# A fused attention, expert and feed-forward kernel: everything from the second expert on written twice, with smaller static blocks in the copy that a flag from the token counts picks

## Chip, cores and metric

The kernel runs on one core of one Trainium2 chip. The metric is device time in microseconds (us). One core has TensorE (PE; its weight loads are shown as PEld), VectorE (DVE), ScalarE (ACT), GpSimd (POOL), SyncE (SP, which issues transfers here) and 16 DMA engines. [...]

## What is computed

Attention with a threshold, then a layer of eight experts in which every token goes to one expert, then a gated feed-forward network. Cut to what matters here:

```python
scores = scale * q @ k.T                       # 4 batches, 8 heads, 576 tokens, 64 wide
scores = where(scores >= max(scores) - tau, scores, -1e9)
x = (softmax(scores) @ v)                      # -> x: 2304 tokens x 512
logits = x @ w_gate                            # 2304 x 8
expert = argmax(logits, axis=1)
for e in range(8):
    xe = x[expert == e]
    y[expert == e] = prob[expert == e] * (maximum(xe @ w1[e], 0) @ w2[e])   # 512 -> 1024 -> 512
h = y @ w_in                                   # 512 -> 2048
out = (h * sigmoid(1.702 * h)) @ w_out         # 2048 -> 512
```

How many tokens an expert gets is known only when the kernel runs. With the inputs used here the reference's routing gives, sorted, 535, 339, 305, 270, 267, 218, 197 and 173 tokens.

## The kernel before

**Stages.** `attention` runs first and also does the gate. Its last steps, in `count` (which calls `routing` and `offsets`), sort the experts by their number of tokens: rank 0 is the expert with most. While attention still runs, the kernel picks the expert that leads so far and does its first 256 tokens as rank 0's first block (`first_ops`); `Moe1.ahead` prepares the remaining `CAPS[0] - FIRST` = 304 columns of rank 0. Then `Moe1.plan` does those 304 columns and one block for each of ranks 1 to 7, and `Moe2.plan` the feed-forward network in six blocks of 384 tokens.

**Static blocks.** Matmul widths are fixed when the program is built. Rank r has a block of `CAPS[r]` columns: 544, 448, 376, 336, 312, 288, 264, 256. Columns beyond the tokens that are there are padding rows. If a rank has more tokens than its block, a general path (`general`) adds further blocks of 256 in a loop; the value `trip`, computed in `offsets` and loaded into a register of every engine by `load_trip`, says whether it is needed. `tc.If(trip > 0)` stands between attention and `Moe1.plan`, and here every engine jumps over its body.

**One block.** Each weight and activation is split in two parts, high and low (type float32r, `F32R`), and every product is done as three matmuls (high x high, high x low, low x high). A block of n columns has 96 matmuls for `x @ w1` (line 1243: 8 chunks of 128 hidden features, 4 input chunks, 3 products) and 96 for `h @ w2` (line 1259), all with a 128 x 128 weight and n columns. A block's tokens come as gathers of 128 rows (`XCH`), each followed by a group of four transposes on TensorE (line 1234) and two copies (`put_x`). Weights of an expert come as eight pieces of 512 KB (`load_w`, line 1224) through three buffers `wraw`; ScalarE copies the high part (line 1389) and VectorE subtracts for the low part (line 1393): a split. `reg_op` and `idx_op` fetch a rank's expert number, offset and index list on SyncE. In the free time of the other engines 32 jobs convert `w_in` from 64-bit numbers (`wi_job`, `convert64`), as 16 more convert `w_out` in the second network.

**Order.** The whole order is written out by hand through a planner (`Plan`): each operation has an engine, a cost, a key and dependencies. `Plan.order` always takes the operation that can start first, by the costs given, and the smaller key where two can start at once; rings (`pl.ring`) stand for buffers. The operations are then emitted in that order, and each engine works through its own list strictly in order. All of attention, `ahead` and `first_ops` are one such list, all of `Moe1.plan` and `Moe2.plan` another. An `If` splits lists: nothing of one side can be moved past it, and each engine passes it when it gets there.

**Memory.** In `moe_kernel` the pools `ht`, `w0`, `xt`, `y`, `wiraw`, `cv`, `cv1` and `w1` serve the experts and are closed (`c2.close`) when `Moe2.open` opens its own: `wo2`, `yg` (four buffers for x loads), `cv2`, `x2_p`, `wo1`, `gp` and `t`. Outputs leave through three buffers `xg`, one indirect scatter of 128 rows at a time on GpSimd (line 1676).

Of the kernel before, what the change touches and what calls it, by code (L numbers as in the profile page):

```python
# [22 lines left out]
SEG = 2560  # L23
TBR = E * SEG
CAPS = [544, 448, 376, 336, 312, 288, 264, 256]
XW = 2 * NT + 256
# [21 lines left out]
class Plan:  # L48
# [11 lines left out]
    def op(self, eng, cost, key, fn, deps=(), take=None, free=None, lat=None, after=(), halves=False):  # L60
# [11 lines left out]
        return o  # L72

# [934 lines left out]

XCH = [[min(o, c - 128) for o in range(0, c, 128)] for c in CAPS]
XCH[0] = [min(o, CAPS[0] - 128) for o in range(FIRST, CAPS[0], 128)]  # L1010
NBLK = [[(0, 256), (FIRST, CAPS[0] - FIRST)]] + [[(0, c)] for c in CAPS[1:]]
HW = max(n for bl in NBLK for _, n in bl)
TB = 384
NC_CONST = 8 * 3 + 9 + 64 + 8


def shape_consts():
# [7 lines left out]
    c[:, 97] = BIG / 8  # L1025
    c[:, 33:97] = (np.arange(8)[None, :] < np.arange(8)[:, None]).reshape(64)
# [61 lines left out]
def offsets(nc, st, sm):  # L1088
# [19 lines left out]
    nc.vector.tensor_reduce(trip, nb, axis=AX.X, op=ALU.max)  # L1108
    before = sm.tile([128, E, E], F32, name="before")
# [16 lines left out]
    st.update(offi=offi, trip=trip, nbi=nbi, row0=row0, col0=col0)  # L1126


def load_trip(nc, st):
    st["trip_v"] = nc.values_load(st["trip"][0:1, 0:1], min_val=0, max_val=7)  # L1130
# [132 lines left out]
class Moe1:  # L1263


    def __init__(self, nc, st, ex):
        self.nc, self.st, self.ex, self.P = nc, st, ex, ex.P
        self.regs, self.offs, self.raws, self.wts = {}, {}, {}, {}
        self.idx, self.xgs, self.xts, self.xt, self.h = {}, {}, {}, {}, {}
        self.ops, self.all_st = {}, []  # L1270

# [3 lines left out]
    def w(self, r, which, k):  # L1275
        return self.wts[(r, which, k)] if r else self.st["first"]["w"][(which, k)]
# [12 lines left out]
    def idx_op(self, pl, r, key, deps):  # L1289
        nch, r0, dma = len(XCH[r]), XCH[r][0], self.nc.sync.dma_start  # L1290
        full = (CAPS[r] - r0) // 128
        rows = lambda: self.st["tb"][bass.ds(self.reg(r) * SEG + r0, CAPS[r] - r0)]

# [4 lines left out]
        def part():  # L1298
            dma(self.idx[r][:, full, :], rows()[CAPS[r] - r0 - 128 : CAPS[r] - r0])
# [22 lines left out]
    def ahead(self, pl, bank_of, tiles, h_op):  # L1322
# [5 lines left out]
        n = NBLK[0][1][1]  # L1328
        ops[("x", 0)] = []
        prev = []  # L1330
        for i in range(len(XCH[0])):
            self.gather_op(pl, 0, i, key, st["all_stores"])
            x, r0 = XCH[0][i], XCH[0][0]
# [29 lines left out]
    def plan(self, pl, wi_job, after):  # L1363
        nc, st, ex, P, ops = self.nc, self.st, self.ex, self.P, self.ops
        K = KEYS1
        self.offs[0] = 0
        for name, n in (("w0", 4), ("w1", 4), ("xt", 1), ("y", 3), ("wiraw", 2), ("cv", 2), ("cv1", 1)):
            pl.ring(name, n)
        pl.banks = {k: [(i,) for i in range(8)] for k in "THY"}
        pl.psum = [max(pl.now["ACT"], pl.now["DVE"])] * 8  # L1370
        bank = lambda t, n: self.banks[t["k"][0]][:, 0:n]
        T = T0 = pl.now["PE"]
        prev_y, stores, ids_prev = {}, [], []
        blocks = [NBLK[0][1]] + [b[0] for b in NBLK[1:]]
        times = []
        for off, n in blocks:
            times.append((T, T + 96 * n / 2400 + 0.25))
            T += 192 * n / 2400 + 0.5

        def split(r, which, k):  # L1380
# [20 lines left out]
        def put_x(r, i):  # L1401
            t = times[r][0]
            tx, tp = ops[("xt", r)], {}
            if ("gather", r, i) not in ops:
                self.gather_op(pl, r, i, t - K["G"], [])
            x, r0 = XCH[r][i], XCH[r][0]
# [6 lines left out]
            def hi():  # L1413
                if i == 0:
                    xt = self.xt[r] = [P["xt"].tile([128, 4, HW], F32R, name=nm) for nm in ("xh", "xl")]
# [19 lines left out]
        o_off = pl.op("ACT", 0.3, times[6][0], last_off)  # L1435

        for r, (off, n) in enumerate(blocks):
            last = r == E - 1
# [3 lines left out]
            if r:  # L1442
# [4 lines left out]
                for k in range(4):  # L1447
                    split(r, 0, k)
            if r:
                ops[("xt", r)] = {}  # L1450
                for i in range(len(XCH[r])):
                    put_x(r, i)
# [5 lines left out]
            for fc in range(8):  # L1458
# [5 lines left out]
                def h_hi(fc=fc, tp=tp, r=r, n=n):  # L1464
                    self.h[r][fc] = [P["ht"].tile([128, HW], F32R, name=f"{p}{fc}")[:, 0:n] for p in ("hh", "hl")]
# [61 lines left out]
            def ids(r=r):  # L1527
                src = st["tb"][bass.ds(self.reg(r) * SEG, CAPS[r])]
                nc.sync.dma_start(st["tbc"][bass.ds(self.offs[r], CAPS[r])], src)

            ids_prev = [pl.dma(ty + 14 * c, 0.1, [ids], [ops[("reg", r)]] + ids_prev, after=[o_y])]

        before, late = pl.ops[:first_y], pl.ops[first_y:]
# [11 lines left out]
def general(tc, nc, st, w):  # L1545
# [7 lines left out]
    with tc.If(st["trip_v"] > 0), ExitStack() as c:  # L1553
        pool = c.enter_context(tc.tile_pool(name="gen", bufs=1))
        ps = c.enter_context(tc.tile_pool(name="ps_g", bufs=2, space=PSUM))
        with tc.For_i(0, E, 1) as r:
            reg, row0, col0 = load("kidx", r, E - 1), load("row0", r, (E - 1) * SEG + CAPS[0]), load("col0", r, NT + CAPS[0])
            nb = nc.values_load(st["nbi"][0:1, bass.ds(r, 1)], min_val=0, max_val=7)
            with tc.For_i(0, nb, 1) as k:
# [10 lines left out]
                for i in range(2):  # L1570
# [4 lines left out]
                    t_ps = ps.tile([128, 4, 128], F32, name="gt")  # L1575
# [4 lines left out]
                for fc in range(8):  # L1580
                    h_ps = ps.tile([128, 256], F32, name="ghp")
# [5 lines left out]
                for dc in range(4):  # L1587
                    y_ps = ps.tile([128, 256], F32, name="gyp")
# [6 lines left out]

class Moe2:
    def __init__(self, tc, nc, st, banks, wi_t, wo, out, raw_p, o_p):
        self.tc, self.nc, self.st, self.banks, self.wi_t, self.wo, self.out = tc, nc, st, banks, wi_t, wo, out
        self.raw_p, self.o_p = raw_p, o_p
        self.xgs, self.x2, self.raws, self.th, self.g, self.ot = {}, {}, {}, {}, {}, {}  # L1600
        self.ids = st["cst"].tile([128, NT // 128, 2], I32, name="ids")

    def open(self, ctx):
        for name, bufs in (("wo2", 1), ("yg", 4), ("cv2", 2), ("x2_p", 1), ("wo1", 1), ("gp", 3), ("t", 2)):
            setattr(self, name, ctx.enter_context(self.tc.tile_pool(name=name, bufs=bufs, reuse_waits="tile")))
        self.wo_t = {}
        for p, Fs in ((self.wo2, range(8, 16)), (self.wo1, range(8))):
            for F in Fs:
# [278 lines left out]
```

## Time and profile before

| what | value |
|---|---|
| timed runs: median (lowest to highest of 3) | 977.88 us (977.53 to 980.33) |
| profiled execution: its own time | 984.31 us |
| profiled execution: span, first to last instruction | 982.6 us |
| granted TensorE clock, mean over the span | 0.987 |
| TensorE busy | 954.6 us, 97% |
| VectorE, ScalarE, GpSimd busy | 562.9, 529.7 and 411.2 us |
| bytes moved by DMA | 106.90 MB, 109 GB/s on average |

The profile is one execution; its time is a little above the timed runs. "Busy" of an engine is time in which it had an instruction under way; waiting and issuing transfers don't count. Matmuls overlap, so that a single one's duration is longer than the distance from one to the next.

### The profile page before, as it was taken

How to read it: one execution, taken by the hardware profiler on the slowest of the kernel's cores; microseconds unless marked ns; L12 is line 12 of the kernel's file. 1: busy time of each engine (PE TensorE's matmuls, PEld its weight loads, DVE VectorE, ACT ScalarE, POOL GpSimd, SP SyncE). 2: the span in 40 equal slices, each digit the busy share in tenths (PEclk: the TensorE clock that was granted, in tenths of full speed). 3: DMA queues.
4: the chain of work that ended last, by engine and by line, in shares of the span. 5: the costliest groups of instructions: out<-in, count | busy, mean ns of one | idle time of the engine just before them, and what ended most of it. 6: DMA issues, size and time to landing. Idle time of an engine off the chain costs nothing.

```text
span 982.6 us, 16924 instructions
## 1 busy us (share of the span) xinstructions
PE 954.6 (97%) x6204; PEld 864.9 (88%) x6205; DVE 562.9 (57%) x1189; ACT 529.7 (54%) x1170; POOL 411.2 (42%) x455
## 2 busy tenths in 40 slices
PE   7998999999989899999999999999999999999996
PEld 5888888888879899999999998999999999999995
DVE  6886888888856347888995488882411111111111
ACT  5886889889854345766675465543322322322221
POOL 6979978845275213555450000001432422522321
PEclk7999999999989999999999999999999999999999
DMA  8723532300243567877776373300200100000000
GB/s 309 223 88 109 162 108 79 108 22 22 58 137 108 171 197 217 257 214 235 241 223 212 116 220 86 106 24 13 95 22 1 54 11 1 33 0 1 33 1 33
DMA packets 50551, 106.90 MB, mean 109 GB/s; under 512 B 12816, under 2 KB 22032, under 8 KB 49936
## 3 DMA queue, kind: packets, MB, share of 16 engines
q1 hardware_dynamic: 45632, 93.43, 30.4%
q0 software_dynamic: 4096, 11.56, 3.8%
q8 instruction: 50, 0.82, 0.4%
q10 hardware_dynamic: 736, 0.79, 0.2%
q14 instruction: 37, 0.30, 0.1%
HBM read 87.37 MB, written 18.57 MB: 108 GB/s over the span
## 4 chain that ended last, share of the span: by engine, by line
PE 61%; DVE 2%; DMA 2%; issue 1%; ACT 0%; POOLq 0%; SPq 0%; DVEq 0%; ACTq 0%
PE b L1639 21%; PE b L1666 20%; PE b L1259 12%; PE b L1243 9%; DVE wlo L1393 1%; DMA wraw<-in_w 1%; PE b L1234 1%; DMA out<-xg,ids 1%; DVE hl L1250 0%; ACT whi L1389 0%; POOLq L1883 0%; DVE wil L1172 0%; ACT xg L1671 0%; ACT yt L1504 0%; ACT hh L1247 0%
## 5 line engine op out<-in xcount | busy, mean ns | idle before, releaser
L1648 DVE SCALAR_TENSOR_TENSOR th<-th,b 128x384 f32<-128x384 f32 x96 | 53.1, 553 | 250.1 <-ACT th L1644 250.1
L1644 ACT ACTIVATE th<-b 128x384 f32<-128x384 f32 x96 | 47.2, 492 | 201.9 <-PE b L1639 198.8
L1639 PE MATMUL b<-x2h,wil 128*128 128x384 f32 x384 | 129.5, 337 | 0.0
L1639 PE MATMUL b<-x2h,wih 128*128 128x384 f32 x384 | 129.3, 337 | 0.0
L1639 PE MATMUL b<-x2l,wih 128*128 128x384 f32 x384 | 128.9, 336 | 0.0
L370 DVE TENSOR_REDUCE nm<-pair 128x1 f32<-128x576 f32 x144 | 107.0, 753 | 27.8 <-PE pair L360 26.2
L389 DVE SCALAR_TENSOR_TENSOR pt<-pair,thr,et 128x576 f32<-128x576 f32 x144 | 114.3, 813 | 13.3 <-ACT et L378 12.3
L1659 POOL TENSOR_TENSOR gl<-th,gh 128x384 fp32r<-128x384 f32 x60 | 61.0, 1017 | 140.1 <-ACT gh L1656 136.3
L1666 PE MATMUL b<-woh,gl 128*128 128x512 f32 x276 | 109.2, 396 | 0.0
L1666 PE MATMUL b<-wol,gh 128*128 128x512 f32 x276 | 109.0, 395 | 0.0
L1666 PE MATMUL b<-woh,gh 128*128 128x512 f32 x276 | 107.3, 389 | 0.0
L378 ACT ACTIVATE et<-pair,nm 128x576 f32<-128x576 f32 x144 | 107.3, 745 | 0.0
L411 ACT COPY ptT<-bank 128x512 f32<-128x512 f32 x144 | 81.3, 589 | 25.4 <-PE bank L405 25.1
L1393 DVE TENSOR_TENSOR wlo<-wraw,whi 128x1024 fp32r<-128x1024 f32 x56 | 75.9, 1375 | 27.1 <-ACT whi L1389 24.1
L405 PE MATMUL bank<-ident,pt 128*128 128x128 f32 x576 | 86.1, 283 | 4.3 <-DVE pt L389 3.3
L1623 POOL TENSOR_TENSOR x2l<-xr,x2h 128x384 fp32r<-128x384 f32 x16 | 16.1, 1033 | 170.5 <-ACT x2h L1619 170.5
L360 PE MATMUL pair<-kst,qh 128*128 128x288 f32 x320 | 84.9, 348 | 1.3 <-DVE kst L285 0.6
L405 PEld LDWEIGHTS bank<-ident,pt 128*128 128x128 f32 x576 | 68.5, 145 | 17.3 <-ACT thr L374 6.2
L1639 PEld LDWEIGHTS b<-x2h,wih 128*128 128x128 f32 x384 | 72.2, 188 | 4.2 <-DVE th L1648 0.3
L1639 PEld LDWEIGHTS b<-x2l,wih 128*128 128x128 f32 x384 | 72.1, 188 | 3.9
L1639 PEld LDWEIGHTS b<-x2h,wil 128*128 128x128 f32 x384 | 72.0, 188 | 0.0
L1259 PE MATMUL b<-hh,whi 128*128 128x448 f32 (+6 forms) x224 | 71.4, 319 | 0.1
(256 smaller groups left out, 2309.6 us busy)
## 6 DMA issues: line engine op xcount, KB each, us to landing
wraw<-in_w SPq DMA_DIRECT2D x64, 512.0 KB, 4.7
qraw<-in_qd SPq DMA_DIRECT2D x40, 256.0 KB, 4.0
wiraw<-in_wi SPq DMA_DIRECT2D x32, 256.0 KB, 4.0
wraw<-in_wo SPq DMA_DIRECT2D x16, 512.0 KB, 3.6
kraw<-in_kd SPq DMA_DIRECT2D x14, 576.0 KB, 4.6
vt<-in_vf SPq DMA_DIRECT2D x4, 1024.0 KB, 7.6
xn<-xt SPq DMA_DIRECT2D x16, 256.0 KB, 3.2
xr<-x2t SPq DMA_DIRECT2D x20, 192.0 KB, 2.7
```

The costliest lines, as they stand in the source:

```text
L360: nc.tensor.matmul(s_ps[:, n, 0:288], w, ks[bb][:, h, 288 * n : 288 * n + 288], start=(i == 0), stop=(i == len(seq) - 1),)
L370: nc.vector.tensor_reduce(t["nm"], t["s"][:, :, 0:288], axis=AX.XY, op=ALU.max, negate=True)
L378: nc.scalar.activation(t["e"], t["s"][:, :, 0:288], AF.Exp, bias=t["nm"], scale=1.0)
L389: nc.vector.scalar_tensor_tensor(pt[:, 576 * x : 576 * x + 576].rearrange("p (n k) -> p n k", n=2), t["s"][:, :, 0:288], t["thr"][:, 0:1], ...
L405: nc.tensor.transpose(t["t"][:, c, :], pt[:, o : o + 128], ident)
L411: nc.scalar.copy(blk["ptT"][:, 4 * x : 4 * x + 4, 128 * ci : 128 * ci + 128], t["t"])
L1243: self.nc.tensor.matmul(h_ps, ww[:, o : o + 128], xx[dc], start=(k == 0), stop=(k == 11))
L1259: self.nc.tensor.matmul(y_ps, w[:, o : o + 128], h, start=(k == 0), stop=(k == 23))
L1393: nc.vector.tensor_tensor(w[1], self.raws.pop((r, which, k)), w[0].bitcast(F32), op=ALU.subtract)
L1639: self.nc.tensor.matmul(h_ps, w[:, dc, :], x[:, dc, :], start=(k == 0), stop=(k == 11))
L1659: eng.tensor_tensor(self.g[n][1], self.th.pop(n), self.g[n][0].bitcast(F32), op=ALU.subtract)
L1666: self.nc.tensor.matmul(o_ps, g[:, cs], w, start=(F == 0 and k == 0), stop=(F == 15 and k == 2))
```

## The change

From rank 1 on, the program stands twice. A second list of widths, `FEW`, is smaller than `CAPS` for all ranks but rank 0. `offsets` computes a flag `more`, which is 1 if any rank has more tokens than `FEW` holds; `load_trip` loads it into a register of every engine in place of `trip`. Rank 0's 304 columns are planned and emitted once, together with what begins rank 1 (its index list, the splits of its first projection and three of its gathers). Then `tc.If(more < 1)` chooses: the first arm plans ranks 1 to 7 and the second network with `FEW`; the other arm first has the general path (moved here from its place after attention) and then the same with `CAPS`. For this, `Plan.fork` and `Moe1.fork` copy the planner's state.

The buffers `ht`, `w0` and `xt` now live from rank 0 to the end, and the second network uses them again: `w0` holds the converted `w_out` of the first eight chunks, `xt` and half of `ht` the two x blocks, the rest of `ht` the gated activations (four buffers instead of three). Its x loads use the three `xg` buffers in place of four of their own.

```diff
+FEW = [544, 384, 344, 320, 304, 280, 256, 232]
...
+    def fork(self):
+        p = copy.copy(self)
+        p.ends = {k: dict(v) for k, v in self.ends.items()}
+        p.ops, p.caps, p.count = list(self.ops), dict(self.caps), dict(self.count)
+        p.psum, p.now = list(self.psum), dict(self.now)
+        p.banks = dict(self.banks)
+        return p
...
+def chunks(caps):
+    return [[min(o, c - 128) for o in range(0 if r else FIRST, c, 128)] for r, c in enumerate(caps)]
...
     nc.vector.tensor_reduce(trip, nb, axis=AX.X, op=ALU.max)
+    nc.vector.tensor_tensor(rest, n, shc[:, 105:113], op=ALU.subtract)
+    over = sm.tile([128, 1], F32, name="over")
+    nc.vector.tensor_reduce(over, rest, axis=AX.X, op=ALU.max)
+    more = cst.tile([128, 1], I32, name="more")
+    nc.vector.tensor_scalar(more, over, 0.0, None, op0=ALU.is_gt)
...
-    st["trip_v"] = nc.values_load(st["trip"][0:1, 0:1], min_val=0, max_val=7)
+    st["more_v"] = nc.values_load(st["more"][0:1, 0:1], min_val=0, max_val=1)
...
-                w = [P[f"w{which}"].tile([128, 1024], F32R, name=x) for x in ("whi", "wlo")]
+                w = [P["w1"].tile([128, 1024], F32R, name=x) for x in ("whi", "wlo")] if which else self.w0[k]
...
-        for name, bufs in (("wo2", 1), ("yg", 4), ("cv2", 2), ("x2_p", 1), ("wo1", 1), ("gp", 3), ("t", 2)):
+        for name, bufs in (("cv2", 2), ("t", 2), ("wo_p", 1)):
...
-        raw = self.yg.tile([128, TB], F32, name="xr")
+        raw = self.o_p.tile([128, DM], F32, name="xg")[:, 0:TB]
...
-        general(tc, nc, st, ex.w)
...
+        def begin(pl, split, put_x):
+            m1.idx_op(pl, 1, 0.0, [])
+            for k in range(4):
+                split(1, 0, k)
+            for i in range(3):
+                put_x(1, i)
+
+        with ExitStack() as c:
+            P["y"] = c.enter_context(tc.tile_pool(name="y0", bufs=3, reuse_waits="tile"))
+            for name, n in (("w0", 4), ("xt", 1), ("y", 3)):
+                pl.ring(name, n)
+            m1.plan(pl, [0], begin)
...
+        with tc.If(st["more_v"] < 1) as fits:
+            with ExitStack() as c:
+                rest(c, pl.fork(), m1.fork(FEW))
+        with fits.Else():
+            general(tc, nc, st, ex.w, banks)
+            with ExitStack() as c:
+                rest(c, pl.fork(), m1.fork(CAPS))
```

`rest` holds what `moe_kernel` did before from the pools of `w_in` on: it opens the remaining pools, defines `wi_job` and `after`, and calls `m1.plan(pl, range(1, E), None, wi_job, after)`.

## Rows read from the trace of the kernel before

**Rows 1.** The page: busy us (share of the span) x instructions.

```profile
PE 954.6 (97%) x6204; PEld 864.9 (88%) x6205; DVE 562.9 (57%) x1189; ACT 529.7 (54%) x1170; POOL 411.2 (42%) x455
```

**Rows 2.** Stretches: length, busy of PE, PEld, DVE, ACT, POOL, clock, DMA.

```profile
361.83:549.09 187.26, 185.83 (x1222) 181.84 (x1221) 150.72 (x273) 119.48 (x234) 76.19 (x78) 1.00 0.73 228
467.78:497.56 29.78, 29.13 (x207) 28.78 (x206) 27.67 (x49) 20.55 (x42) 16.32 (x15) 1.00 0.80 243
572.29:973.87 401.58, 401.58 (x2016) 363.62 (x2015) 134.13 (x250) 136.02 (x270) 95.70 (x95) 1.00 0.13 39
```

**Rows 3.** The chain that ended last, from 357 us: start, us, what, count.

```profile
357.00 5.00 PE b L1259 x36
361.99 19.46 PE b L1243 x96
...
391.18 0.44 PE b L1234 x4
...
402.22 16.63 PE b L1243 x96
...
462.42 5.54 PE b L1259 x36
...
490.85 6.88 PE b L1259 x48
...
498.93 3.44 DVE wlo L1393 x2
...
517.38 7.90 PE b L1259 x60
525.28 11.52 PE b L1243 x96
...
549.25 11.51 PE b L1243 x96
...
861.02 2.10 PE b L1639 x12
```

**Rows 4.** Timeline of PE near 290 us: start, us, line, operation, shape, count.

```profile
289.57 1.02 PE L478 MATMUL pair<-iw,aoT 128*128 128x144 f32 x7
290.42 0.60 PE L405 MATMUL bank<-ident,pt 128*128 128x128 f32 x4
```

**Rows 5.** Timeline of PE in rank 0's block, idle time before in brackets.

```profile
333.87 0.86 PE L1243 MATMUL b<-kraw,qraw 128*128 128x304 f32 x5 [0.33 <-issue]
...
344.98 0.82 PE L1243 MATMUL b<-kraw,ql 128*128 128x304 f32 x4 [1.19 <-DVE hl L1250]
```

**Rows 6.** Timeline of SP, 337 to 364 us.

```profile
337.79 0.34 SPq L1224 DMA_DIRECT2D wraw<-in_w  x1
...
338.96 0.33 SPq L1224 DMA_DIRECT2D wraw<-in_w  x1
...
362.88 0.42 SPq L1508 DMA_DIRECT2D x2a<-yt  x1
```

**Rows 7.** Timeline of DVE in the offsets.

```profile
311.41 0.16 DVE L1108 TENSOR_REDUCE trip<-nb 128x1 int32<-128x8 f32 x1
```

**Rows 8.** Waits of PE, 318 to 575 us: in total, times, longest.

```profile
PE b L1243 <- ACTq L1553: 0.6, 1, 0.6
```

**Rows 9.** Transfers by line: count, KB each, median us to landing.

```profile
wraw<-in_w SPq DMA_DIRECT2D x64, 512.0 KB, 4.7
...
out<-xg,ids POOLq DMA_INDIRECT x18, 2.7
```

**Rows 10.** The line of the old `If`: duration ns min/median/max.

```profile
L1553 POOLq INC_SWDGE_SEM  x1: 654/654/654, 323.4 to 323.4; - x1
```

**Rows 11.** Timeline of POOL from 955 us.

```profile
975.65 0.96 POOL L1676 DMA_INDIRECT out<-xg,ids  x1 [2.52 <-DMA out<-xg,ids]
```

**Rows 12.** The line that closes the program: duration ns min/median/max, first to last.

```profile
L1883 POOLq DRAIN  x3: 40/113/6332, 975.4 to 982.3; - x3
```

**Rows 13.** The page, DMA queues: packets, MB, share of 16 engines.

```profile
q8 instruction: 50, 0.82, 0.4%
```

More of the change, by code (lines that the diff above doesn't have):

```diff
@@ L1 @@
+import copy
 from contextlib import ExitStack
@@ L1270, in __init__, with sized, fork @@
         self.ops, self.all_st = {}, []
+    def sized(self, caps):
+        self.CAPS, self.XCH = caps, chunks(caps)
+    def fork(self, caps):
+        m = copy.copy(self)
+        for k, v in vars(self).items():
+            if isinstance(v, (dict, list)) and k != "P":
+                setattr(m, k, copy.copy(v))
+        m.sized(caps)
+        return m
     def reg(self, r):
@@ L1433, in last_off @@
             self.last_off = nc.scalar.value_load(src, min_val=0, max_val=NT)
-        o_off = pl.op("ACT", 0.3, times[6][0], last_off)
+        if after:
+            o_off = pl.op("ACT", 0.3, times[6][0], last_off)
         for r, (off, n) in enumerate(blocks):
+            if r not in ranks:
+                continue
             last = r == E - 1
@@ L1447, in plan @@
                 for k in range(4):
-                    split(r, 0, k)
+                    if ("split", r, 0, k) not in ops:
+                        split(r, 0, k)
             if r:
-                ops[("xt", r)] = {}
-                for i in range(len(XCH[r])):
-                    put_x(r, i)
+                for i in range(len(self.XCH[r])):
+                    if ("put", r, i) not in ops:
+                        put_x(r, i)
             if r:
@@ L1700, in load_x @@
                 ty = {}
-                ld = pl.dma(t - 4, 0.55, [lambda q=q: self.load_x(b, q)], store_ops if b else stores, take=("yg", ty), after=prev)
+                ld = pl.dma(t - 4, 0.55, [lambda q=q: self.load_x(b, q)], store_ops if b else stores, take=("xg", ty), after=prev)
                 prev = [ld["src"]]
@@ L1729, in plan @@
             tp, tt, tg = {}, {}, {}
-            spare = b == NB - 1 and F >= 12
+            spare = max(F - 12, 0) if b == NB - 1 else 0
             o = pl.op(
@@ L1818, in after @@
-        def after(pl, before, stores, store_ops, last_y, ids_op, T):
-            def opened():
-                c2.close()
-                m2.open(c3)
-            o = pl.op("SEQ", 0.0, 0, opened, after=before)
-            m2.plan(pl, T, o, stores, store_ops, last_y, ids_op)
-        m1.plan(pl, wi_job, after)
+        keep = lambda name: ctx.enter_context(tc.tile_pool(name=name, bufs=1, reuse_waits="tile"))
+        ht, w0, xt = keep("ht"), keep("w0"), keep("xt")
+        m1.h_t = [[ht.tile([128, HW], F32R, name=f"{x}{k}") for x in ("hh", "hl")] for k in range(8)]
```

176 lines of the change are left out of this document (103 added, 73 removed).

## The prediction

> **What bounds the kernel now.** I read the page first, for the engines' shares: TensorE is busy in nearly all of the span, no other engine in much over half [rows 1]. Then the busy times by stretch, cut where the blocks of one expert begin [rows 2]: from 361.83 to 572.29 us, which is 210.46 us, TensorE works through the seven blocks of ranks 1 to 7, and the last 401.58 us after that are the second network without an idle stretch. [...] A busy TensorE need not be at its pace, so I read the chain that ended last for that: its rows count matmuls and give the time of each run of them, and a run of 96 is one projection of one block [rows 3]. From these come the periods by width: 448 columns 19.46/96 = 202.7 ns, 376 173.2, 336 153.9, 312 143.3, 304 138.9, 288 131.7, 264 120.0, 256 119.9, and 384 (the second network) 175.0. Seven blocks of 192 matmuls at these periods are 192 x 1044.7 ns = 200.6 us; 17 groups of four transposes at 0.44 us, done between them for the next block, are 7.5 us. That makes 208.1 of 210.46 us: about 2.4 us are stalls. So this stage is set by columns through TensorE, and only there can smaller blocks pay. VectorE is the near second: 150.72 us of the 187.26 us up to the last block, and 27.67 of 29.78 in one block [rows 2].
>
> **The change part by part.** Which copy runs: by the reference's own routing the tokens sorted by expert are 535, 339, 305, 270, 267, 218, 197, 173. Each fits its place in FEW (544, 384, 344, 320, 304, 280, 256, 232), so the flag is 0 and the copy with the smaller blocks should run.
>
> *Matmuls.* Rank 0 keeps its width. The widths in between I take on a line between neighbouring rows [rows 3]: 344 gives 157.8 ns, 320 146.8, 280 127.8. Saved per matmul: 448 to 384 27.7 ns; 376 to 344 15.4; 336 to 320 7.1; 312 to 304 4.4; 288 to 280 3.9; 264 to 256 0.1; 256 to 232 taken as nothing. The sum is 58.6 ns x 192 = 11.25 us. The last two I count at (nearly) nothing because 264 and 256 columns run at the same 120 ns, and because seven 144-column matmuls, with the same 128 x 128 weights to load for each, take 0.85 us, 121 ns each [rows 4]: below some 260 columns the period does not follow the width. On the line of the wider rows (0.4 ns a column) 232 would give 110 ns and 1.9 us more; that is the gain end. [...]
>
> *Transposes.* 448 and 264 columns need one group of four more than 384 and 256: two groups, 0.87 us [rows 3]. TensorE altogether: 12.1 us less.
>
> *The first part.* The branch around the general path, which all engines took between the attention and rank 0, is gone from there. After it TensorE stood 0.33 us with no releaser, and later 1.19 us for VectorE [rows 5]. That wait is a late load. VectorE sat on the split of rank 1's last piece of weights, whose load SyncE issued only at 337.79 us [rows 6], since it fetches the registers and index lists of ranks 2 to 5 ahead of it; these now stand behind the new branch. Both can go: -1.5 us, at the other end nothing. Against it three small VectorE operations for the flag stand before the offsets that SyncE waits for; at the 0.16 us of such a reduction and a step of some 0.2 us each [rows 7] they cost 0.6 us, or nothing where the lists' landing covers them. I take -1.2 in all.
>
> *The new branch.* All engines pass it between rank 0 and rank 1. What TensorE lost to the old one, which jumps, was 0.6 us [rows 8]. The copy with few columns is the first arm, so no jump is needed, and matmuls are queued on TensorE. 0 to 0.6 us, taken as 0.3.
>
> *Loads moved behind the branch.* Before, SyncE issued loads for rank 1's second projection from 338.96 us on, during rank 0, and they lay in their buffers when rank 1 began [rows 6]. Now only the first projection is fetched ahead; SyncE first issues rank 0's last stores (362.88 + 0.42 us), passes the branch, loads two registers and two lists for rank 2, and only then rank 1's other weights: about 366 us instead of 340. A load takes 4.7 us to land [rows 9], a split, by its VectorE half of 1.72 us [rows 3] and a ScalarE half before it, some 2.7 us more. Three buffers hold three loads, so the fourth can go out near 373 us and be split near 380. Rank 1's second projection starts at 361.8 + 96 x 0.175 = 378.6 us and wants that fourth piece 2.1 us later. So the cover is nearly used up: 0 if it just holds, 3 us if each step is late by one operation; I take 1.0.
>
> *VectorE.* Its work up to the last block falls by about 2 us (160 columns less in eight operations, one copy less) to 149 us, while the stretch shrinks by 12 us to 175: 80% becomes 85%, and the wi conversions start some 7 us later. The chain already runs through its splits (one piece is 3.44 us for two [rows 3]), and the fullest block, 29.78 us long, holds 192 x 143.3 ns + 3 x 0.44 us = 28.8 us of work, so it lost 1.0 us there. If the five middle blocks each lose that, stalls grow from 2.4 to 5 us; if no more than before, by 0; if all seven lose it and the late loads come on top of each, by some 5 us. I take 2.5.
>
> *The second network.* It reads the same number of columns, at 175 and 231 ns. Its x loads now share three buffers with the outputs instead of having four; the fourth load of its second block goes out only after the first is split. One load (2.7 us) and split later with some 2 us of cover: 0 to 2 us, taken as 0.5.
>
> *The end.* After its last work each engine has to jump over the other copy and to bring semaphores level first. Nearest rows: the old join cost GpSimd 0.65 us for one such update [rows 10]. The last scatter is issued at 975.65 us [rows 11] and lands 2.7 us later [rows 9], and the last drain ends at 975.4 + 6.33 = 981.8 us [rows 12], 3.4 us after that. If all this now runs after the update the end is 4.5 us later, if the drain covers it nothing. I take 1.5. [...]
>
> Sum: -12.1 - 1.2 + 0.3 + 1.0 + 2.5 + 0.5 + 1.5 = -7.5 us. Against the profiled execution's 984.31 us that gives 976.8; the median of the timed runs, 977.88, lies 6.4 us lower, and with the same difference it becomes 970.4 us.
>
> **The rivals.**
> 1. *TensorE alone counts.* Stalls stay as they are, the end is covered: -12.1 - 1.2 = -13.3, 964.6 us. For it: the second network's 401 us without a gap and a stage that lost only 2.4 us of 210. Against it: VectorE at 93% in one block.
> 2. *VectorE or the late loads take the place.* At the upper ends of both, 5 us for VectorE (2.5 more than taken) and 3 us for the loads (2 more), a gain of 3.0 us is left: 974.9 us; with one of them at its end 973. For it: the wait at 344.98 us [rows 5], and chains through the splits; against it: its slack after 525 us.
> 3. *The join costs more than an update.* If the jump waits for three instruction packets (3.8 us) on top of the 4.5 us, the end costs 8.3 instead of 1.5 us: 977.2 us, no difference. For it: packets take 1.26 us each [rows 13], and the other copy is long. Against it: the old branch, a short jump, shows only 0.33 us [rows 5]. [...]
> [...]
> 5. *The flag picks the old widths.* Then the program only gains the joins and the second branch: 978 to 981 us. It needs a rank with more tokens than FEW; the tightest are rank 0 with 9 and rank 2 with 39 to spare.
>
> **How the numbers follow.** A measurement of this kernel can tell some 0.3%, 2.9 us. Chances: the forecast (967 to 973) 52%, rival 1 17%, rival 2 (973 to 977) 13%, rival 3 10%, rival 4 5%, rival 5 3%. Faster by over 0.3% (below 975.0): the first two and half of rival 2, 75%. Within 0.3%: the other half, and rival 3, 17%. Slower: rivals 4 and 5, 8%. The range leaves out rivals 4 and 5, the far half of 3 and the gain of a cheap 232-column block: 963.5 to 976.5 us.
>
> **What the profile after would show.** Blocks of 384, 344, 320, 304, 280, 256 and 232 columns; the stretch from rank 1's first matmul to the second network some 198 to 202 us long instead of 210.46. The 256- and 232-column blocks both at 120 ns. No idle TensorE near 334 and 345 us. The loads for rank 1's second projection at 366 us, and a wait for a split, if any, near 379 us. The second network unchanged at 401 to 402 us. From the last scatter's issue to the end 8 to 9 us, 7 before. I am wrong if the expert stretch hardly shrinks (VectorE's waits in its place), if the 232-column block has a longer period than the 256-column one, or if the end grows by more than 5 us.

## The result and the profile after

The changed kernel takes 969.87 us (median of 4 runs, 966.13 to 970.39), the kernel before, on the same chips, 979.11 us (977.53 to 982.78). The ratio is 0.9881, 95% interval 0.9845 to 0.9916: 8 to 15 us faster. The profile of the kernel before, 984.31 us, is slower than all four of these timed runs, so the two profiles show a larger gain than the timed runs do. The flag picked the smaller widths.

The page of the changed kernel, to be held against [rows 1]:

```profile
PE 937.9 (97%) x6196; PEld 849.4 (88%) x6197; DVE 552.0 (57%) x1190; ACT 524.6 (54%) x1168; POOL 414.7 (43%) x453
```

Busy times by stretch (columns as in [rows 2]): rank 0's block, ranks 1 to 7, the second network. Below them the same of the kernel before, cut at the second network's first matmul (the prediction cut at its second, 0.17 us later).

```profile
329.17:357.87 28.70, 28.51 (x204) 28.29 (x205) 10.97 (x19) 10.13 (x19) 4.13 (x3) 1.00 0.25 80
357.87:558.12 200.25, 196.75 (x1410) 193.99 (x1409) 156.30 (x296) 126.08 (x256) 82.64 (x80) 1.00 0.76 240
558.12:957.43 399.31, 399.31 (x2018) 362.04 (x2016) 129.85 (x245) 135.06 (x269) 96.11 (x95) 1.00 0.12 38
```

```profile
331.27:361.83 30.56, 29.03 (x208) 28.66 (x209) 12.03 (x19) 11.28 (x20) 7.52 (x7) 1.00 0.57 165
361.83:572.12 210.29, 208.86 (x1414) 204.87 (x1413) 160.95 (x291) 128.81 (x255) 76.19 (x78) 1.00 0.70 218
572.12:973.87 401.75, 401.75 (x2018) 363.79 (x2016) 134.30 (x250) 136.19 (x270) 95.70 (x95) 1.00 0.13 39
```

The expert stretch is 10.0 us shorter, rank 0's block 1.9, the second network 2.4, and from the last matmul to the end of the span it takes 10.7 us (968.1 - 957.43) where it took 8.7 (982.6 - 973.87). The span is 14.5 us shorter; the other 2.1 us lie ahead of rank 0 (329.17 against 331.27). They are there after the first 25 us, in attention code that is the same: the same four transposes begin at 24.96 us before and at 22.81 us after. The granted clock, a share of the full one, differed there, as the same stretch of both shows (third number from the right), before and after:

```profile
10.00:25.00 15.00, 11.12 (x59) 9.76 (x59) 11.77 (x22) 8.90 (x21) 13.48 (x14) 0.66 1.01 347
```

```profile
10.00:25.00 15.00, 10.80 (x70) 9.33 (x71) 12.89 (x26) 10.35 (x24) 14.17 (x14) 0.89 1.03 349
```

Before, it stood at 0.50 in every stretch of 2 us from 12 to 22 us; after, it was back at 1.00 from 18 us on. So these 2.1 us belong to the two executions and not to the change.

Look at TensorE's busy time in the expert stretch: 3.5 us of idle time now, 1.4 before. And look at the DMA share, the second number from the right: in rank 0's block it fell from 0.57 to 0.25, after it rose from 0.70 to 0.76. That is the load of weights that moved.

The first projections (96 matmuls each) of the blocks of 384, 320, 280, 256 and 232 columns, from the first start to the next projection's first start:

```profile
357.87:374.52 16.65, 16.65 (x98) 16.65 (x97) 7.16 (x13) 7.96 (x15) 2.83 (x3) 1.00 0.71 226
427.37:441.45 14.08, 14.08 (x99) 14.08 (x97) 14.05 (x26) 11.67 (x25) 5.35 (x5) 1.00 0.82 263
485.34:497.60 12.26, 12.26 (x98) 12.26 (x97) 8.27 (x16) 8.65 (x17) 3.43 (x4) 1.00 0.84 265
512.62:524.13 11.51, 11.51 (x98) 11.51 (x97) 10.45 (x17) 7.98 (x18) 6.48 (x4) 1.00 0.68 206
536.68:547.40 10.72, 10.72 (x98) 10.72 (x97) 6.43 (x11) 4.78 (x10) 0.00 (x0) 1.00 0.74 237
```

Divided by 96 these are 173.4, 146.7, 127.7, 119.9 and 111.7 ns a matmul. The last one was predicted at 120.

TensorE's waits in the expert stretch (total us, times, longest):

```profile
PE b L1277 <- DVE xl L1457: 1.5, 3, 0.7
PE b L1252 <- DVE hl L1268: 1.5, 1, 1.5
PE b L1261 <- DVE hl L1268: 0.3, 1, 0.3
```

All name VectorE. But follow the longest one, which ended with the `hl` of 500.28 us, back through the timelines of ACT and DVE:

```profile
495.15 1.05 ACT L1422 CAST wh<-wraw 128x1024 fp32r<-128x1024 f32 x1 [2.32 <-DMA wraw<-in_w]
...
496.23 1.23 DVE L1426 TENSOR_TENSOR wl<-wraw,wh 128x1024 fp32r<-128x1024 f32 x1 [1.94 <-PE b L1261]
...
500.28 0.44 DVE L1268 SCALAR_TENSOR_TENSOR hl<-b,hh 128x280 fp32r<-128x280 f32 x1
```

ScalarE stood 2.32 us for a weight load that had not landed, and VectorE behind it had nothing to do. (The split's row names a matmul, but the `wh` that it reads was finished by ScalarE at 495.15 + 1.05 = 496.20 us, 0.03 us before the split began.) Then both had a backlog of splits and conversions ahead of the `hl` that the next transposes' bank waited for. In this wait VectorE is where the delay passes through, not where it begins.

### The profile page after: what moved, and what is told of

Read it like the earlier page. It is cut to its first block, busy times and chain, and to the rows that moved or that the text cites. A ratio compares the mean times of both kernels' runs of the same rounds, so it can differ in the third digit from the quotient of the medians.

```text
span 968.1 us, 16904 instructions
## 1 busy us (share of the span) xinstructions
PE 937.9 (97%) x6196; PEld 849.4 (88%) x6197; DVE 552.0 (57%) x1190; ACT 524.6 (54%) x1168; POOL 414.7 (43%) x453
## 5 line engine op out<-in xcount | busy, mean ns | idle before, releaser
L1277 PE MATMUL b<-hh,whi 128*128 128x384 f32 (+6 forms) x224 | 69.2, 309 | 1.5 <-DVE xl L1457 1.5
L370 PE MATMUL pair<-kst,ql 128*128 128x288 f32 x320 | 69.5, 299 | 0.3 <-DVE ql L337 0.3
L1261 PE MATMUL b<-xh,wh 128*128 128x384 f32 (+6 forms) x224 | 67.7, 302 | 0.3 <-DVE hl L1268 0.3
L1277 PE MATMUL b<-hh,wlo 128*128 128x384 f32 (+6 forms) x224 | 67.6, 302 | 0.0
L1277 PE MATMUL b<-hl,whi 128*128 128x384 f32 (+6 forms) x224 | 67.6, 302 | 0.0
L1261 PE MATMUL b<-xl,wh 128*128 128x384 f32 (+6 forms) x224 | 67.6, 302 | 0.0
L1261 PE MATMUL b<-xh,wl 128*128 128x384 f32 (+6 forms) x224 | 67.6, 302 | 0.0
L442 PE MATMUL bank<-ptT,vt 128*64 128x256 f32 (+1 forms) x656 | 67.0, 348 | 0.5 <-ACT ptT L430 0.5
L1698 PE MATMUL b<-hh,wil 128*128 128x384 f32 x192 | 64.7, 337 | 0.0
L1698 PE MATMUL b<-xh,wil 128*128 128x384 f32 x192 | 64.6, 337 | 0.0
## 6 DMA issues: line engine op xcount, KB each, us to landing
xg<-x2t SPq DMA_DIRECT2D x20, 192.0 KB, 2.4
```

The source lines that it names most:

```text
L370: nc.tensor.matmul(s_ps[:, n, 0:288], w, ks[bb][:, h, 288 * n : 288 * n + 288], start=(i == 0), stop=(i == len(seq) - 1),)
L442: nc.tensor.matmul(blk["o"][64 * x : 64 * x + 64, lo:hi], vfull[bb][:, c, 2 * blk["hp"] + x, :], blk["ptT"][:, 4 * x + c, lo:hi], start=(c ...
L1261: self.nc.tensor.matmul(h_ps, ww[:, o : o + 128], xx[dc], start=(k == 0), stop=(k == 11))
L1277: self.nc.tensor.matmul(y_ps, w[:, o : o + 128], h, start=(k == 0), stop=(k == 23))
L1698: self.nc.tensor.matmul(h_ps, w[:, dc, :], x[dc], start=(k == 0), stop=(k == 11))
```

## The experiments

Lines of the code are those of the changed kernel, in rows of the one-copy programs those of the kernel before. For each program the stretches of its profile, cut as above, and the timed median with its ratio to the kernel before. The kernel before, run beside each group of programs, had medians of 979.11 to 981.59 us, so the ratio compares two programs better than their medians do.

| program | rank 0 | ranks 1 to 7 | second network | last matmul to end | median, us | ratio (95%) |
|---|---|---|---|---|---|---|
| before | 30.6 | 210.3 | 401.8 | 8.7 | 979.11 | 1 |
| changed | 28.7 | 200.3 | 399.3 | 10.7 | 969.87 | 0.9881 (0.9845 to 0.9916) |
| few_one_copy | 29.0 | 195.4 | 401.7 | 8.9 | 963.56 | 0.9850 (0.9827 to 0.9872) |
| wide_two_copies | 31.6 | 212.6 | 399.3 | 11.5 | 984.31 | 1.0051 (1.0031 to 1.0071) |
| wil_on_gpsimd | 28.6 | 204.8 | 399.3 | 12.0 | 971.05 | 0.9905 (0.9882 to 0.9928) |
| few_one_copy_late | 29.9 | 201.0 | 401.7 | 8.9 | 971.90 | 0.9895 (0.9848 to 0.9941) |
| light_wi | 30.1 | 198.7 | 399.3 | 11.8 | 965.76 | 0.9821 (0.9775 to 0.9868) |
| early_loads | 30.1 | 198.0 | 399.3 | 11.0 | 967.38 | 0.9855 (0.9812 to 0.9899) |
| early_lists | 29.2 | 198.7 | 399.3 | 8.5 | 963.24 | 0.9822 (0.9782 to 0.9862) |
| one_arm_384 | 28.6 | 199.2 | 399.3 | 8.5 | 965.10 | 0.9843 (0.9805 to 0.9882) |
| early_wi | 30.1 | 196.4 | 399.3 | 10.7 | 965.10 | 0.9844 (0.9808 to 0.9879) |
| tight | 30.2 | 192.0 | 400.3 | 10.9 | 959.59 | 0.9815 (0.9780 to 0.9850) |
| tight_early | 30.1 | 195.7 | 399.3 | 10.7 | 962.58 | 0.9808 (0.9767 to 0.9849) |
| tight_one_copy | 30.5 | 189.4 | 401.8 | 8.5 | 954.43 | 0.9709 (0.9661 to 0.9756) |

The expert stretch of the same order of work differs by about 1 us between executions (200.3 and 199.2 us in the changed kernel and one_arm_384, the only such pair), and rank 0's block, with the same matmuls in all programs with two copies, by 3 us.

**Columns alone, and structure alone.** The first program is the kernel before with the smaller widths, the second the changed kernel with the old ones.

```diff
-CAPS = [544, 448, 376, 336, 312, 288, 264, 256]
+CAPS = [544, 384, 344, 320, 304, 280, 256, 232]
```

> The kernel before, still one copy with its branch ahead of rank 0, but with the smaller widths as its only ones (544, 384, 344, 320, 304, 280, 256, 232). Theory, that the change pays by columns alone and that the new stalls come with VectorE having less time: rank 1 to second network falls from 210.46 us to 200 to 201, as in the changed kernel (200.25); rank 0's block stays at 30.6 us, the second network at 401.6, the end after the last matmul at 8.7; in all 9 to 10 us faster than before, ratio about 0.990. Rival, that the new stalls come from the loads behind the new branch: there is no such branch here, the stretch is 196 to 197 us, ratio about 0.986. By the prediction's own price the 232-column block would save nothing; by the 112 ns that the changed kernel shows it is 21.5 us long here too.

```diff
-FEW = [544, 384, 344, 320, 304, 280, 256, 232]
+FEW = [544, 448, 376, 336, 312, 288, 264, 256]
```

> The changed kernel with the smaller widths set back to 448, 376, 336, 312, 288, 264, 256 in the copy that runs: both copies, the flag, the branch and the shared buffers stay, no column is saved. Theory (columns pay, VectorE brings the stalls): rank 0's block about 28.7 us (30.56 before), rank 1 to second network 210.5 to 211.5 (210.46), second network 399.3 (401.58), end after the last matmul 10.7 (8.73); together 1 to 2 us faster than before, not to be told from no change. Rival (the late loads bring the stalls): the stretch grows to 213 to 214 us and the whole is 1 to 2 us slower than before.

The expert stretches of the one and the other:

```profile
353.86:549.24 195.38, 194.52 (x1410) 194.06 (x1409) 158.97 (x290) 126.88 (x255) 75.71 (x77) 1.00 0.73 232
```

```profile
358.22:570.84 212.62, 210.58 (x1412) 204.54 (x1413) 166.18 (x299) 129.71 (x257) 79.93 (x81) 1.00 0.73 230
```

Columns alone take 14.9 us off the stretch, and 0.9 us of idle TensorE is left. This kernel's median is 6.3 us below the changed one's; by the ratios it is 3 us, and their intervals overlap. The structure alone makes the kernel 0.5% slower (3 to 7 us): 2.3 us in the stretch, 2.7 at the end and 1.1 in rank 0's block, at a clock of 0.95 there, against 2.4 gained in the second network. So in the stretch of the changed kernel the columns brought some 15 us and the structure took some 5 back. The first run bears out the rival, the second is nearer to it. The new stalls do not come with narrower blocks alone: TensorE is idle 0.9 us in the stretch with narrow blocks in one copy, 2.0 with wide blocks in two, and 3.5 with both (1.4 before). The second copy costs 2.3 us at the old widths and 4.9 at the new ones, so its price is not fixed. Of these 4.9 us, 2.6 are idle rows; the rest are shorter delays between matmuls that the busy time covers (at 383.14 us in the changed kernel, for one, the next row begins 0.48 us later where the usual step is 0.17). VectorE has the same work in 195 us in few_one_copy (158.97 us, 81%), and keeps up.

**Less VectorE work.** The last step of the `w_in` conversions goes to GpSimd.

```diff
-        nc.vector.tensor_tensor(lo, c["lf"], hi.bitcast(F32), op=ALU.subtract)
+        eng.tensor_tensor(lo, c["lf"], hi.bitcast(F32), op=ALU.subtract)
```

> The changed kernel with the last step of the 32 w_in conversions (a 128x256 subtraction, 0.41 us on VectorE) on GpSimd: 13 us of VectorE's 156 us in the expert stretch go to an engine that is busy 83 us of 200. Theory (VectorE brings the stalls): the stretch falls from 200.25 to 197 to 198 us. Rival (late loads): 200 us, no change. Third case: GpSimd's own latency (about 0.7 us a step) holds the conversion buffers longer, and wi loads come later; no change or up to 1 us slower.

Its expert stretch, to be held against 200.25 us in the changed kernel:

```profile
353.88:558.68 204.80, 197.55 (x1411) 194.18 (x1409) 163.75 (x264) 127.27 (x256) 113.26 (x112) 1.00 0.74 235
```

The stretch grew to 204.8 us, by more than any theory allowed. But the edit did not relieve VectorE. It took 32 instructions from it (296 to 264), some 14 us, and yet VectorE's busy time rose from 156.3 to 163.8 us, because other steps got longer: those of line 1167 took 526 ns on average where they had taken 339, those of line 1179 411 ns where they had taken 299. GpSimd, which also gathers the tokens, was busy 113.3 us in place of 82.6. So this run does not test VectorE as the bound; that rests on few_one_copy. What lengthened the steps, and which wait made the stretch longer, it does not show.

**Late loads put into the one-copy kernel.** Only the place of rank 1's second-projection loads changes.

```diff
         prev = self.ops.get("load", [])
+        if (r, which) == (1, 1):
+            prev = prev + self.ops["y0"]
```

> The one-copy kernel with the smaller widths (963.56 us; 195.38 us from rank 1 to the second network), in which one thing is changed: the four loads for rank 1's second projection may be issued only after rank 0's last matmul has been put in order, so they stand behind rank 0's last stores on SyncE, as in the changed kernel. No second copy, no branch there, no shared buffers. Theory, that the 5 us by which the changed kernel's expert stretch is longer (200.25 against 195.38) come from these loads: three pieces of 512 KB move from rank 0's block, where the DMA engines are then 25% busy in place of 57%, into a stretch that moves 250 GB/s; 1.5 MB at that rate are 6 us, and the stretch grows to 199 to 201 us. Rival (branch, order and buffers of the second copy are the cause): it stays at 195 to 196 us.

The stretch grew by 5.6 us, and the timed ratio is 0.9895, like the changed kernel's (its interval still overlaps few_one_copy's a little). Most of it lies here, at rank 2's start, in two rows of TensorE's timeline and in stretches of 2 us:

```profile
387.32 0.66 PE L1234 MATMUL b<-ident,xg 128*128 128x128 f32 x4 [1.19 <-DMA xg<-xn,it]
389.84 0.65 PE L1243 MATMUL b<-xh,whi 128*128 128x344 f32 x1 [1.86 <-DVE xl L1424]
```

```profile
385.00:387.00 2.00, 1.13 (x8) 0.86 (x7) 2.00 (x5) 0.76 (x2) 1.84 (x2) 1.00 0.96 349
387.00:389.00 2.00, 0.66 (x4) 0.42 (x4) 1.08 (x1) 1.17 (x2) 1.67 (x3) 0.94 0.77 200
389.00:391.00 2.00, 1.16 (x4) 1.16 (x5) 1.74 (x3) 1.27 (x5) 1.77 (x3) 0.50 0.98 305
391.00:393.00 2.00, 2.00 (x9) 2.00 (x8) 2.00 (x6) 1.03 (x4) 1.51 (x1) 0.50 0.87 299
393.00:395.00 2.00, 2.00 (x9) 2.00 (x8) 2.00 (x6) 1.17 (x2) 1.38 (x2) 0.50 0.94 297
395.00:397.00 2.00, 2.00 (x13) 2.00 (x12) 1.24 (x1) 0.51 (x2) 0.16 (x1) 0.86 0.91 302
```

The DMA engines are 0.77 to 0.98 busy, a gather of rank 2's tokens comes late while weights are loaded, TensorE stands 1.19 and then 1.86 us, and its granted clock falls to 0.50: 9 matmuls in 2 us instead of 13. The clock is back in the stretch from 395. So of the 5.6 us 2.4 are added idle time (3.3 us in the stretch against 0.9) and 3.2 added busy time, most of it from the clock. The changed kernel has the same lateness in another form, several shorter waits at a clock of 1.00; that the two losses, 5.6 and 4.9 us, are so near each other is partly chance.

**Fewer bytes.** In the changed kernel, `raws` keeps the first two `w_in` pieces, which all jobs convert.

```diff
+                    n = 256 if j < 2 else 32
+                    t = c["raw"] if j < 2 else P["wisink"].tile([128, 32, 2], I32, name="wisink")
-                    nc.sync.dma_start(c["raw"], src[:, 512 * k : 512 * k + 512].rearrange("p (n t) -> p n t", t=2))
+                    nc.sync.dma_start(t, src[:, 512 * k : 512 * k + 2 * n].rearrange("p (n t) -> p n t", t=2))
```

> The changed kernel with 30 of the 32 w_in loads cut from 256 KB to 32 KB each; the conversions all run, on the data of the first two loads (so the second network works with wrong weights). 6.9 MB fewer of the about 48 MB that pass in the expert stretch, and VectorE, ScalarE and GpSimd have the same work. Theory that the late loads cost because the DMA engines are near their limit there: stretch 195 to 197 us in place of 200.25. Rival, late by latency and order alone: the waits for rank 1's and 2's weights stay, 199 to 201 us. VectorE as the bound: 200 us.

198.7 us: 1.5 us less, hardly more than the 1 us by which the same order differs. In this profile most of the loss stays with 14% fewer bytes, at DMA engines that are 0.67 busy, which speaks against their being simply full. But the profile is the slowest of the program's four runs (969.47 us, the others 962.15 to 965.87), so the run does not settle it.

**The loads put back.** In `begin`, ahead of the branch, in the changed kernel; the three `wraw` buffers become tiles that live through both arms.

```diff
             for i in range(3):
                 put_x(1, i)
+            for k in range(3):
+                m1.load_op(pl, 1, 1, k, 2000.0 + k)
```

> The changed kernel with both copies, and the first three loads for rank 1's second projection issued ahead of the branch (the three load buffers are tiles that live through both arms). Theory (late loads): the DMA share of rank 0's block goes from 0.25 back to about 0.55, the expert stretch from 200.25 to 195 to 196 us, the second network stays at 399.3 and the end at 10.7: 5 us faster than the changed kernel, 964 to 966 us. Rival (branch and order): the stretch stays at 199 us or more.

The next program also fetches the lists of ranks 2 to 5 ahead, and has no other arm.

```diff
+            for r in range(2, 6):
+                m1.reg_op(pl, r, 3000.0 + r)
+                m1.idx_op(pl, r, 3000.0 + r, [])
```

> The changed kernel with the three early loads, in which also the registers and index lists of ranks 2 to 5 are fetched ahead of the branch, as before the change. The other arm (general path and wide blocks) is left out of the program, since these lists have the narrow blocks' offsets; its counts are not served. Theory (what is left of the longer stretch, 198.04 against 195.38 us, is the rest of SyncE's work behind the branch): the stretch falls to 195 to 196 us. Rival (order of the planner's list from the branch on, or smaller buffers): 198 us. The end after the last matmul: 8.7 to 8.9 us as with one copy if the jump over the other arm and the levelling of semaphores made it 10.7 to 12; about 10.7 if the closing of an arm alone does. Rank 0's block 28.6 to 30.1 us, second network 399.3.

The third is early_loads with earlier due times for `wi_job`.

```diff
+        T0 -= 192 * (self.CAPS[0] - FIRST) / 2400 + 0.5
         gap = K["WE"] * (T - T0) / 32
```

> Both copies with the three early loads, in which the planner's due times of the 32 w_in conversions are counted from rank 0's start, as before the change, and not from rank 1's: they come about 25 us earlier at first and 12 us earlier in the middle, at the same work. In the one-copy kernel with the smaller widths GpSimd's part of them is over before the last two blocks (3.23 and 0 us busy), in the changed kernel 8.82 us stand in the last block but one. Theory (what is left of the longer stretch, 198.04 against 195.38 us, is that they crowd the middle): 195.5 to 196.5 us, 964 us in all. Rival: 198 us or more; what is left lies in the order that the planner finds from the branch on, or in buffers, and stays open.

The stretches of the three, in this order:

```profile
355.69:553.73 198.04, 195.76 (x1411) 194.10 (x1409) 159.69 (x296) 126.51 (x256) 80.39 (x80) 1.00 0.74 235
```

```profile
354.57:553.31 198.74, 195.89 (x1410) 194.28 (x1409) 162.41 (x296) 128.34 (x256) 77.48 (x77) 1.00 0.73 230
```

```profile
356.65:553.00 196.35, 195.13 (x1411) 194.05 (x1409) 161.94 (x296) 127.08 (x256) 82.85 (x80) 1.00 0.74 237
```

Early loads bring 2.2 us of the 4.9 back, earlier conversions another 1.7, both somewhat more than the 1 us by which the same order differs; the lists bring nothing that shows. With early loads alone the stretch, 198.0 us, lies between theory and rival, and the DMA share of rank 0's block came to 0.39, not 0.55. With both, the stretch is within 1 us of the one-copy kernel's. The steps are read from the profiles; the timed intervals of these programs overlap with the changed kernel's, and one_arm_384, with its loads late, has the median of early_wi, so the times alone do not prove them. As far as single profiles show, what was lost is work of the next stage that rank 0's block had carried: first the loads, then the due times of the conversions, which the planner counted from rank 1's start once rank 0 was a list of its own.

**The end and the second network.**

```diff
-HW = max(CAPS[1:])
+HW = max(FEW[1:])
...
-        with fits.Else():
-            general(tc, nc, st, ex.w, banks)
-            with ExitStack() as c:
-                rest(c, pl.fork(), m1.fork(CAPS))
```

> The changed kernel without the other arm, and with the activations' tiles 384 wide in place of 448 (the widest block left). Tests where the second network's 2.4 us come from (399.3 us in all programs with two copies, 401.7 in all with one, with the same matmuls). If from how far apart the x slices lie in memory (384 against 448 columns): 401.7 us. If from the buffers that hold the gated values and x, or their number: 399.3 us. The end: 8.7 to 8.9 us if the other arm makes it longer, 10.7 or more if not. The expert stretch 200 to 201 us, since the loads stay late.

The end is 8.5 us, as in early_lists, the other program without the second arm: the arm costs 2.2 us (programs with it have 10.7 to 12.0 us). GpSimd's branch and drain, first in the changed kernel, then in early_lists (duration ns min/median/max, first to last start):

```profile
L1909 POOLq COMPARE_BRANCH  x2: 40/40/41, 330.9 to 959.7; - x2
L1972 POOLq DRAIN  x3: 40/107/5053, 962.2 to 967.8; - x3
```

```profile
L1917 POOLq COMPARE_BRANCH  x2: 38/39/40, 327.2 to 954.1; - x2
L1976 POOLq DRAIN  x3: 45/112/6003, 954.3 to 960.9; - x3
```

With an arm to jump over, the drain begins 2.5 us after the branch, without one 0.2 us; as the drain itself is 1.0 us shorter then, 1.4 us of that reach the end. In that gap the trace has two packets of 8 KB on an instruction queue, at 960.66 and 960.80 us. Over the whole program the instruction queue has more packets with the arm than without (changed kernel, then early_lists):

```profile
q14 instruction: 42, 0.34, 0.1%
```

```profile
q14 instruction: 34, 0.28, 0.1%
```

The other 0.7 us stand ahead of the last scatter:

```profile
959.81 0.96 POOL L1735 DMA_INDIRECT out<-xg,ids  x1 [3.10 <-POOLq L1909]
```

The scatter waited 3.10 us where [rows 11] show 2.52, and names a semaphore instruction of the branch's line. The second network stays at 399.3 us with slices of 384 columns: their distance is not the cause.

**Widths close to the tokens.**

```diff
-FEW = [544, 384, 344, 320, 304, 280, 256, 232]
+FEW = [544, 344, 312, 272, 272, 224, 200, 176]
```

> The changed kernel with widths close to the numbers of tokens: 344, 312, 272, 272, 224, 200, 176 for ranks 1 to 7. Columns alone, with 158, 143, 124, 124 ns from the line between measured widths and 109 ns (the period of a 128-column transpose in the changed kernel) as floor for the last three: 19 us less than 200.25, so 181 us from rank 1 to the second network and 950 us in all. If VectorE is next (156 us busy of 200 in the changed kernel, 28.84 of 31.36 in its fullest block): blocks of ranks 2 to 4 stay at 27 to 29 us where columns alone would make them 24 to 28, the stretch is 186 to 190 us, and 957 to 960 us in all. [...]

> The kernel before, one copy, with the widths 544, 344, 312, 272, 272, 224, 200, 176. In two copies these widths took 191.97 us from rank 1 to the second network where columns alone would give 181. Late loads as the cause of most of that: 185 to 187 us here, about 953 us in all. DMA throughput as the limit: some 48 MB at most 262 GB/s, the highest rate of a block in the changed kernel, are 183 us, so no lower than that. VectorE as the limit: 190 us or more, as in two copies.

> Both copies, the early loads, and the widths 544, 344, 312, 272, 272, 224, 200, 176 in the copy that runs. With late loads 191.97 us in the stretch, with one copy 189.36. If the late loads explain the difference: 189 to 190 us, 956 us in all. Another bound (VectorE and GpSimd behind weights that arrive at 250 GB/s) is common to all three, so no less than 188.

tight_one_copy is the fastest program of the study, 954.43 us, 2.9% below the kernel before. From its blocks, 96 matmuls of 344 and 96 of 176 columns:

```profile
356.31:371.50 15.19, 15.19 (x98) 15.19 (x97) 12.63 (x25) 12.04 (x24) 3.86 (x4) 1.00 0.83 265
534.40:545.12 10.72, 10.72 (x98) 10.72 (x96) 3.39 (x8) 3.10 (x9) 0.00 (x0) 1.00 0.63 210
```

344 columns take 158.2 ns. 176 take 111.7 ns (10.72/96), to the digit what 232 take. In these rows there is a floor, at 112 ns. But of the 19 us that columns promised only 6.0 came beyond few_one_copy (195.4 to 189.4), with two copies 8.3 (200.3 to 192.0). TensorE is idle 7.4 us in this stretch and its clock 0.98; the waits name `hl`, `xh` and `xl`. With 189.4 us it lies between its two expectations, late loads (185 to 187) and VectorE (190 or more). tight_early, expected at 189 to 190, took 195.7 us in its profile, the slowest of its four runs (966.49 us, the others 960.28 to 963.24); its timed ratio, 0.9808, is that of tight, 0.9815, so with these widths the early loads brought nothing that shows. Which resource sets this pace is left open.

## Why the prediction came out

The total, 970.4 us against 969.87, is closer than its terms. Point by point:

- *Matmuls, -11.25 us: the right mechanism, its size too small.* Measured periods are 173.4 ns (384 columns; the 175.0 of [rows 3] belongs to the second network), 158.2 (344), 146.7 (320), 127.7 (280), 119.9 (256) and 111.7 (232), with 304 as before. Against [rows 3] that is 29.3 + 15.0 + 7.2 + 4.4 + 4.0 + 0.1 + 8.2 = 68.2 ns x 192 = 13.1 us. The interpolated widths were within 0.5 ns. The step that failed is "264 and 256 columns run at the same 120 ns ... below some 260 columns the period does not follow the width": two neighbouring widths and a matmul of another type [rows 4] set the floor 8 ns too high, and 232 columns saved 1.6 us. A row under that floor stood in [rows 3] itself: four transposes, 128 columns each, in 0.44 us are 110 ns apiece. What sets the floor of 112 ns, measured at 232 and 176 columns, no run shows. Rival 4, that the 232-column block is slower, did not come: 111.7 ns a matmul against 119.9 at 256 columns. The two groups of transposes fell away as predicted, one of them in rank 0's block.
- *VectorE, +2.5 us: failed.* In few_one_copy narrower blocks brought no stalls; TensorE's idle time in the stretch fell from 1.4 to 0.9 us. The share of busy time had risen, as worked out, and cost nothing.
- *Loads behind the branch, +1.0 us: the right cause, the price too low.* In the timelines of SP and DVE of the changed kernel

```profile
362.29 0.99 SPq L1242 DMA_DIRECT2D wraw<-in_w  x2
...
376.35 1.23 DVE L1426 TENSOR_TENSOR wlo<-wraw,whi 128x1024 fp32r<-128x1024 f32 x1 [0.48 <-ACT whi L1422]
```

  the first load goes out 4.4 us after rank 1's start (4.2 predicted), and the fourth split ends at 376.35 + 1.23 = 377.58 us with no wait of the second projection for it: the cover just held, as at the prediction's lower end. The step that failed stopped there. It priced the wait for that one piece, and not the loads and conversions queued behind: the first wait that shows came at 389 us, for the copies of rank 2's tokens, and the longest, at 499 us, still goes back to a load (that this one is late because of rank 1's is inferred). Late loads alone cost 5.6 us in one copy, about half of it by the lower clock; loads and conversions brought forward gave back 3.9 of 4.9 in two.
- *First part, -1.2 us: not shown.* The profile has -1.9 us in rank 0's block: 0.4 for the group of transposes, and 1.3 of idle time (1.5 before, 0.2 after). But the same matmuls took 28.6 to 31.6 us in the other programs, with a clock of 0.94 or 0.95 in those of 30 us and more, and few_one_copy, 29.0 us, has no wait like the 1.19 us of [rows 5] although its branch is the old one. No part of the edit in the idle time can be told.
- *The new branch, +0.3 us:* nothing; TensorE goes from 304 to 384 columns without an idle row.
- *Second network, +0.5 us: wrong sign.* It got 2.4 us shorter in every program with the shared buffers but tight, where it got 1.5 us shorter. The buffers were not late; the matmuls are faster (last section).
- *The end, +1.5 us:* 1.9 in the profile, 2.2 against one arm. From the branch to the drain it took 2.5 us, with two instruction packets in that time; whether the jump waited for them is not shown. Rival 3, three packets on top of everything (1.26 us each: 0.4% of 16 engines' 982.6 us over the 50 packets of [rows 13]), did not come.

Against the profiled execution of before the sum was -7.5 us, and -14.5 came, 2.1 of it in the first 25 us, where nothing was changed; by the timed ratio it is 8 to 15. Columns were worth 2 to 3 us more than said (13.1 for 11.25 us by the periods; with the transposes 14.9 for 12.1 in the stretch of few_one_copy), VectorE cost nothing where 2.5 us were put, and the second network gained 2.4 where it was to lose 0.5; against that, late loads and what queued behind them cost 4.9 us for 1.0. Errors of both signs made the total look better than the steps: that it came within 1 us is luck. Rival 2 had the late loads as a case, priced at 3 us at most.

## What to carry to other kernels

A branch put between two stages also cuts the prefetch that crossed it: price not only the first late transfer but the whole chain that runs behind it, and look at what the earlier stage carried for the later one, loads and due times. When a second copy is meant to allow smaller blocks, run the smaller blocks in one copy first: that told the gain (15 us) from the cost of the structure (5 us) in one run. The price of the structure, though, grew from 2.3 to 4.9 us with the smaller blocks. When work is moved off an engine, read its busy time again: here it rose, from 156.3 to 163.8 us. A wait that names an engine is followed back until an engine is found that waits for a transfer.

## What was not expected of the hardware

The same 12 matmuls of 128x384 in the second network run at two paces. First before, then in the changed kernel, start us of consecutive rows:

```profile
643.40 0.34 PE L1639 MATMUL b<-x2h,wil 128*128 128x384 f32 x1
643.57 0.35 PE L1639 MATMUL b<-x2h,wih 128*128 128x384 f32 x1
643.76 0.34 PE L1639 MATMUL b<-x2l,wih 128*128 128x384 f32 x1
643.93 0.34 PE L1639 MATMUL b<-x2h,wil 128*128 128x384 f32 x1
644.12 0.33 PE L1639 MATMUL b<-x2h,wih 128*128 128x384 f32 x1
```

```profile
649.92 0.34 PE L1698 MATMUL b<-xh,wil 128*128 128x384 f32 x1
650.09 0.34 PE L1698 MATMUL b<-xh,wih 128*128 128x384 f32 x1
650.26 0.34 PE L1698 MATMUL b<-xl,wih 128*128 128x384 f32 x1
650.44 0.34 PE L1698 MATMUL b<-xh,wil 128*128 128x384 f32 x1
650.61 0.34 PE L1698 MATMUL b<-xh,wih 128*128 128x384 f32 x1
```

Before, the fourth and sixth matmul after the change from 512 to 384 columns are followed after 0.19 us (643.57 to 643.76, 643.93 to 644.12), the others after 0.17 or 0.18. Over all such groups of the second network these two steps average 0.185 and 0.181 us, the others 0.172 to 0.178; with the shared buffers all average 0.173 to 0.174. The 2.4 us over some 90 such changes are 27 ns each. It is the same whether VectorE or GpSimd works beside it (0.184 and 0.185 us after the fourth matmul, 0.182 us with either after the sixth); with the shared buffers the second network takes 399.3 us with slices 384 or 448 apart; the cause, the buffers' places or their number, was not settled.

In few_one_copy_late a wait of 1.19 us and one of 1.86 us, with one group of transposes between them, went with some 6 us at a granted clock of 0.50 (from 389 into the stretch from 395), which cost about as much as the waits themselves.
